# Joined q/k/v/dO loads, two PSUM copies moved from ACT to DVE, a delayed tail, and stores issued two jobs behind their transposes

## The chip, the cores and the metric

The kernel runs on one core of a Trainium2 chip. The metric is the device time of one execution in microseconds; the table below gives the median of several runs and the time of the one execution that the profiler recorded. The engines are PE (matmul), DVE (vector), ACT (scalar), POOL and SP. SP computes nothing here: it issues DMAs, in order. POOL and, at the start and the end, ACT issue DMAs as well. Work moves between engines by semaphores, and every engine runs its own list in order.

## The reference

The reference computes the sum of a residual, a self-attention block and a SwiGLU block, all on the same layer-normalised input, and then the gradients of everything for a given output gradient. With S = 2048 rows, D = 448 columns, H = 16 heads of 28 and F = 1792:

```python
xn = layernorm(x)                                   # (2048, 448)
q, k, v = split(xn @ wqkv)                          # 16 heads of 28
p = softmax(q @ k.T * 28 ** -0.5)                   # per head 2048 x 2048
A = merge(p @ v) @ wo
B = (silu(xn @ w_gate) * (xn @ w_up)) @ w_down
y = x + A + B
# outputs: y and, for grad_out, the gradients of x, wqkv, wo, w_gate, w_up, w_down
```

## The kernel before

The program has three stages, each with an order of work that is written out by hand.

**Forward stage.** Heads are padded from 28 to 32 rows, so that four heads make a group of 128 partitions and there are G = 4 groups. The loop runs over 256 steps (group, 512 query columns, 128 key rows). In each step PE makes the scores of four heads (L599), ACT takes the exponential (L604), and PE multiplies the one of the step before with v (L581). What time PE has left is filled by `fill(pace)`, which takes small pieces of work from a queue of jobs (`queue`, `cur`): the SwiGLU block and its backward (`ffn_items`), the weight gradients (`dW_items`), the projections of the next group (`proj_items`), and what follows a finished block of outputs (`o_items`). Each piece has a cost, and the pace is the cost that is left divided by the steps that are left. `push(..., front=True, behind=n)` puts jobs into the queue behind its first n jobs.

Many results are needed in a second layout. It is made by a transposing DMA, which SP issues (`sp.dma_start_transpose`), mostly followed by a store to a DRAM buffer. The store waits for the transpose to land. In `o_items` the store of oT is issued by SP right behind its transpose (L493), and the stores of dOT (L524) and of the weight gradients dw_o (L370, L371) are issued by POOL right behind theirs. While an engine's queue waits for a landing, all that is behind it in that queue waits too: on SP the next transposes, on POOL the stores of the SwiGLU rows (L421) and the weight loads of the next block (L161). `proj_done` stores q, k and v transposed into `qT_d`, `kT_d` and `vT_d`, one store of 128 rows each.

**Backward stage.** Heads are taken in NPR = 8 pairs. There are N = 512 units (pair, 512 keys, 128 queries). A window is eight units that share keys, called by W; the place in the window is `pos`, 0 to 7, and the place of a unit is `qi`. In the step of unit k, PE makes the scores of unit k (L851, tile sd), then the products of dO and v of unit k-1 (L862, also sd). ACT makes E of unit k (L869), DVE makes ds of unit k-1 out of sd and E (L880). There are three sd buffers, so the scores of unit k wait for ds of unit k-3, and L862 of unit k waits for E of unit k. Three units late, `acc_mm` (L748) adds up the gradients of k and v. They are taken out by ACT at the end of every second window (dkv_o, L754).

The gradient of q needs ds with queries in the columns (dsT). Of the eight units of a window six are transposed by DMA (L882), and the two in `TQ = (1, 4)` by PE (`pe_transpose`, L775) into the PSUM bank aux: the first at pos 6, copied out by DVE (`tr_out(dve)`, L782), the second at pos 0 of the next window, copied out by ACT (`tr_out(act)`). A ds tile has eight buffers, so the product of unit k may not be written before the readers of unit k-8 are done, its transposing DMA among them.

The aux bank exists once and is passed round. In each window it also takes one *job*: a row block of the output ("y", 19 matmuls), of the gradient of the normalised input ("dx", 14 matmuls), or a part of a weight gradient ("dwq"). The job's matmuls (the `fillers`) are spread over pos 1 to 4, and ACT takes the result out (L727, L691). At pos 5 `dq_mm` (L795) uses the bank for the gradient of q of two windows ago, and DVE takes this out at pos 6 (`dq_out`, L807, L810, L813).

SP's queue in this stage holds the six transposes of a window, two row loads (ck and, for y, x_c) at pos 0, the transposes of dkv_o and dq_o, and the loads of the next pair, the next group and the next weights at pos 4: up to two of the lists `pload` and `wload` and one of `gload` per window. `load_pair` fills the tiles of a pair in half-height pieces: q (rows 0 to 63 of a tile) from `qT_d`, dO (rows 64 to 127 of the same tile) from `dOT_d`, and in the same way k and v. In the loop each piece is half a row long as well, so a pair takes eight loads.

**Tail.** For each of 16 row blocks PE adds up the gradient of the normalised input (14 matmuls, L956 and L958), ACT and DVE make the two sums of the layer norm's backward (L962, L965), and then t1 (ACT, L974), t2 (DVE, L976) and the sum with the residual gradient (POOL, L979), which SP stores (L980).

Of the kernel before, what the change touches and what calls it, by code (L numbers as in the profile page):

```python
# [37 lines left out]
def kernel(  # L38
# [27 lines left out]
    qT_d = dram.tile([G, P, S], BF16, name="qT_d")  # L66
    kT_d = dram.tile([G, P, S], BF16, name="kT_d")
    vT_d = dram.tile([G, P, S], BF16, name="vT_d")
    dOT_d = dram.tile([G, P, S], BF16, name="dOT_d")
# [128 lines left out]
    def proj_done(g):  # L198
# [5 lines left out]
        pool.dma_start(out=vT_d[g], in_=vT[:])  # L204
        pool.dma_start(out=qT_d[g], in_=qT[:])
        pool.dma_start(out=kT_d[g], in_=kT[:])
# [120 lines left out]

    def proj_items(g):
# [15 lines left out]
    def dW_items(fc):  # L344

        out = []
        for wi in range(3):
            box = {}

            def go(t, wi=wi, box=box):  # L350
# [13 lines left out]
                else:  # L364
# [5 lines left out]
                    pool.dma_start(out=dst[0:384].rearrange("(c p) f -> p c f", p=P), in_=o[:, 0:3, :])  # L370
                    pool.dma_start(out=dst[384:448], in_=o[:64, 3, :])  # L371
# [94 lines left out]
    def o_items(g, qc, o_ps):  # L466
# [8 lines left out]
        def tr(i):  # L475
# [3 lines left out]
            if i < 3:  # L479
# [13 lines left out]
            sp.dma_start(out=hd_d[tsl, :, g, :].rearrange("k p s -> p k s"),  # L493
                         in_=oT[:].rearrange("p (k s) -> p k s", k=4))

        def do(i):
# [27 lines left out]
            pool.dma_start(out=dOT_d[g, :, qc * 512:(qc + 1) * 512], in_=dT[:])  # L524
# [20 lines left out]
    def load_pair(pr, parts):  # L545

        g, r = pr // 2, 64 * (pr % 2)
        q = qkp.tile([P, S], BF16, name="qT")
        k = qkp.tile([P, S], BF16, name="kT")
        qd[pr] = (q, k)  # L550
        n = S // parts
        return [lambda i=i, dst=dst, r0=r0, src=src: sp.dma_start(
                    out=dst[r0:r0 + 64, i:i + n], in_=src[g, r:r + 64, i:i + n])
                for r0, srcs in ((0, (qT_d, kT_d)), (64, (dOT_d, vT_d)))
                for dst, src in zip((q, k), srcs) for i in range(0, S, n)]
# [212 lines left out]
    TQ = (1, 4)  # L768
# [9 lines left out]
    def tr_out(eng):  # L778

        ps, dst = st["tr"]  # L780
        out, in_ = dst.rearrange("p j c q -> p (j c) q"), ps[:]
        act.copy(out=out, in_=in_) if eng is act else dve.tensor_copy(out=out, in_=in_)  # L782
# [47 lines left out]
    for k in range(N + 2 * UW):  # L830
        W, pos = k // UW, k % UW
        if k < N:
# [7 lines left out]
            if pos == 4:  # L840
                if W == len(jobs) - 1:
                    wload.extend(load_w("wq", 2))
                for lst, n in ((pload, 2), (gload, 1), (wload, 2)):
# [10 lines left out]
        late_tr = pos == 0 and 1 <= W <= NW  # L854
# [15 lines left out]
        if late_tr:  # L870
            tr_out(act)
# [15 lines left out]
        if pos == 1:  # L887
            if 3 <= k < N + 3:
                acc_mm(k - 3)
            if job:  # L890
                st["aux"] = ps_x.tile([P, 512], FP32, name="aux")
# [120 lines left out]
```

## Time and profile before

| | |
|---|---|
| median of 3 runs | 1534.82 us (1529.53 to 1534.94) |
| the profiled execution | 1534.68 us |
| its span, first to last instruction | 1532.9 us |
| mean granted PE clock over the span | 0.979 |
| PE busy | 1414.2 us (92%) |
| ACT busy | 1187.9 us (77%) |
| DVE busy | 1100.7 us (72%) |
| POOL busy | 395.0 us (26%) |
| first and last product ds | 644.8 and 1455.4 us |

Three kinds of lines are used below. A group line has the source line, the engine, the operation, `out<-in` by the program's names, the count, and busy times; what stands in brackets or at the end is the idle time ahead of it and what ended that. A line of the order of time has start and length in us first. A line of a window view has the window, its length, the busy time and count of each engine, the granted share of PE's clock, the mean busy share of the 16 DMA engines and the GB/s that they moved. Rows with SPq are times in which SP issued a DMA.

### The profile page before, as it was taken

What the parts mean: (1) busy time and instruction counts of PE and PEld (TensorE: products, weight loads), DVE (VectorE), ACT (ScalarE), POOL (GpSimd) and SP (SyncE); (2) the same over time, 40 slices, a digit from 0 to 9 for tenths busy, and PEclk for the clock granted to TensorE, in tenths of its full rate; (3) what the DMA queues carried; (4) which work ended last, traced back from release to release, by engine and by line L of the source; (5) the groups of instructions that cost most, each with busy time, mean ns of one, the idle gap of its engine ahead of it and who ended that gap; (6) DMA issues with size and microseconds to landing.
All of it is one profiled execution on the core that took longest, in us unless ns stands there. A gap on an engine that the chain in (4) does not pass through costs nothing.

```text
span 1532.9 us, 32019 instructions
## 1 busy us (share of the span) xinstructions
PE 1414.2 (92%) x12176; PEld 600.1 (39%) x12176; DVE 1100.7 (72%) x1421; ACT 1187.9 (77%) x1333; POOL 395.0 (26%) x664
## 2 busy tenths in 40 slices
PE   6899999999999999798989988989899899999987
PEld 3233333333333333333334344334345343544353
DVE  7664555656666667377878878888788788888925
ACT  6898998889888888576767777778778778788823
POOL 4332443344435444400111121101112101111033
PEclk9999999999999999889999999999999999999999
DMA  9976767878877799799999999999999999999984
GB/s 216 190 157 144 156 122 157 171 136 169 173 166 144 159 190 214 178 197 208 218 206 207 185 194 209 197 204 206 208 195 197 198 205 183 180 190 211 186 272 140
DMA packets 682106, 285.12 MB, mean 186 GB/s; under 512 B 637136, under 2 KB 650464, under 8 KB 681952
## 3 DMA queue, kind: packets, MB, share of 16 engines
q1 hardware_dynamic: 652016, 210.03, 75.5%
q0 software_dynamic: 25968, 64.53, 17.2%
q10 hardware_dynamic: 3968, 8.52, 1.7%
q8 instruction: 95, 1.56, 0.4%
q14 instruction: 59, 0.48, 0.1%
HBM read 67.34 MB, written 63.44 MB: 85 GB/s over the span
## 4 chain that ended last, share of the span: by engine, by line
PE 59%; ACT 13%; DMA 12%; DVE 8%; issue 6%; POOL 1%; SPq 0%; DVEq 0%; ACTq 0%; POOLq 0%
DMA dsT<-ds 9%; PE f_ps L356 8%; PE s_ps L599 7%; PE f_ps L382 7%; PE sd L851 6%; ACT E L869 5%; PE aux L718 5%; PE acc L748 4%; PE o_ps L581 4%; ACT eT L604 4%; PE aux L775 4%; DVE ds L880 4%; PE aux L795 3%; ACT dsT L782 3%; PE f_ps L180 3%
## 5 line engine op out<-in xcount | busy, mean ns | idle before, releaser
L880 DVE TENSOR_TENSOR ds<-sd,E 128x1024 bf16<-128x1024 f32 x512 | 611.5, 1219 | 134.0 <-PE sd L862 49.8
L869 ACT ACTIVATE E<-sd 128x1024 bf16<-128x1024 f32 x512 | 516.7, 1023 | 175.6 <-PE sd L862 136.5
L604 ACT ACTIVATE eT<-s_ps 128x1024 bf16<-128x1024 f32 x512 | 497.2, 1025 | 79.5 <-PE s_ps L599 76.1
L862 PE MATMUL sd<-kT,qT 32*128 32x512 bf16 x1024 | 203.4, 390 | 22.2 <-ACT E L869 21.3
L851 PE MATMUL sd<-kT,qT 32*128 32x512 bf16 x1024 | 202.7, 392 | 20.6 <-DVE ds L880 18.0
L748 PE MATMUL acc<-ds,v_sp 128*32 128x512 bf16 x1024 | 205.3, 396 | 0.7 <-DVE ds L880 0.7
L748 PE MATMUL acc<-E,O_sp 128*32 128x512 bf16 x1024 | 205.1, 396 | 0.2 <-ACT dkv_o L754 0.2
L599 PE MATMUL s_ps<-qT,kT 32*128 32x512 bf16 x1024 | 152.8, 383 | 10.1 <-ACT eT L604 7.9
L421 POOL DMA_DIRECT2D hd_d<-fT x168 | 126.9, 773 | 18.5 <-DVE fT L416 5.3
L382 PE MATMUL f_ps<-xnT,wgu 128*128 128x512 bf16 x448 | 117.6, 381 | 1.7 <-DVE w_sb L408 1.5
L763 POOL DMA_DIRECT2D dqkv_d<-dkv_o x64 | 39.2, 616 | 293.3 <-ACT dkv_o L754 291.4
L718 PE MATMUL aux<-W,ck 128*128 128x448 bf16 x448 | 107.5, 357 | 3.3
L851 PEld LDWEIGHTS <-qT 32*128 32x128 bf16 x1024 | 51.2, 91 | 150.0 <-issue 141.2
L581 PE MATMUL o_ps<-eT,v_sp 128*32 128x512 bf16 x1024 | 102.8, 391 | 0.0
L356 PE MATMUL f_ps<-xn_sp,f_sp 128*128 128x448 bf16 x448 | 99.7, 356 | 0.0
L599 PEld LDWEIGHTS <-kT 32*128 32x128 bf16 x1024 | 42.4, 90 | 143.5 <-issue 136.8
L748 PEld LDWEIGHTS <-O_sp 128*32 128x32 bf16 x1024 | 50.3, 93 | 113.5 <-issue 104.0
L775 PE MATMUL aux<-ident_bf,ds 128*128 128x128 bf16 x1024 | 81.3, 224 | 13.5 <-DVE dq_acc L807 6.5
L356 PEld LDWEIGHTS <-f_sp 128*128 128x128 bf16 x672 | 58.3, 98 | 78.6 <-issue 23.5
L862 PEld LDWEIGHTS <-qT 32*128 32x128 bf16 x1024 | 65.2, 91 | 60.5 <-issue 56.5
L775 PEld LDWEIGHTS <-ds 128*128 128x128 bf16 x1024 | 63.5, 99 | 42.4 <-issue 41.7
L394 DVE SCALAR_TENSOR_TENSOR g<-t_sb,f_ps 128x512 f32<-128x512 f32 x56 | 38.4, 686 | 54.0 <-ACT t_sb L392 53.9
(133 smaller groups left out, 1763.1 us busy)
## 6 DMA issues: line engine op xcount, KB each, us to landing
hd_d<-fT POOLq DMA_DIRECT2D x168, 128.0 KB, 4.6
ck<-hd_d SPq DMA_DIRECT2D x32, 448.0 KB, 4.3
ck<-hd_d SPq DMA_DIRECT2D x16, 576.0 KB, 4.9
dsT<-ds SPq DMA_TRANSPOSE x384, 4.2
dqkv_d<-dkv_o POOLq DMA_DIRECT2D x64, 64.0 KB, 3.8
dq_c<-dqkv_d ACTq DMA_DIRECT2D x5, 768.0 KB, 6.1
W<-wT_d SPq DMA_DIRECT2D x14, 224.0 KB, 3.6
out_dram<-dw_o POOLq DMA_DIRECT2D x28, 96.0 KB, 3.7
```

The costliest lines, as they stand in the source:

```text
L356: pe.matmul(acc[:, :D], lhsT=src[:, 12 * (t // 4) + 4 * wi + t % 4, :], rhs=rhs[:, t, :D], start=(t == 0), stop=(t == NT - 1))
L382: pe.matmul(st[name][:], lhsT=w(c), rhs=src[:, tsl, c, :], start=(c == 0), stop=(c == 3))
L581: pe.matmul(o_ps[HP * hh:HP * (hh + 1), :], lhsT=v[:, kt, HP * hh:HP * (hh + 1)], rhs=e[hh // 2][:, hh % 2, :], start=(kt == 0), stop=(kt ...
L599: pe.matmul(s_ps[:, j, :], lhsT=kT[r:r + HP, kt * P:(kt + 1) * P], rhs=qT[r:r + HP, qc * 512:(qc + 1) * 512], start=True, stop=True, tile_ ...
L604: act.activation(out=e[:], in_=s_ps[:], func=ACT.Exp, scale=SCALE)
L718: return [lambda n=n: pe.matmul(ps[:, :D], lhsT=t[:, n, :], rhs=w[:, n, :], start=(n == 0), stop=(n == NFC - 1)) for n in range(NFC)]
L748: pe.matmul(acc[r:r + HP, :], lhsT=src[:, qt, 64 * hp + HP * j:64 * hp + HP * j + HP], rhs=m[:, j, :], start=(qt == 0), stop=(qt == NT - 1 ...
L775: pe.transpose(ps[:, i, :], ds[:, i // 4, (i % 4) * P:(i % 4 + 1) * P], ident_bf[:])
L851: pe.matmul(s_ps[:, j, :], lhsT=q[HP * j:HP * j + HP, qt * P:(qt + 1) * P], rhs=kv[HP * j:HP * j + HP, kc * 512:(kc + 1) * 512], start=Tru ...
L862: pe.matmul(d_ps[:, j, :], lhsT=q[r:r + HP, qt * P:(qt + 1) * P], rhs=kv[r:r + HP, kc * 512:(kc + 1) * 512], start=True, stop=True, tile_p ...
L869: act.activation(out=E[k][:], in_=s_ps[:], func=ACT.Exp, scale=SCALE)
L880: dve.tensor_tensor(out=DS[k - 1][:], in0=d_ps[:], in1=E[k - 1][:], op=ALU.mult)
```

## The change

The change has four parts.

1. *Loads.* The buffers `qT_d` and `dOT_d` become one, `qdo_d`, with a tile of 128 rows for each pair (64 of q, 64 of dO); `kT_d` and `vT_d` become `kv_d`. A pair is then loaded by four full-height loads instead of eight. The stores that fill the buffers are split by pairs: `proj_done` issues six instead of three, and dOT takes two instead of one. In the loop, a window of even number issues one load of a pair, one of odd number one load of a group.
2. *Copies.* The units that PE transposes are 2 and 6. Both results are copied out by DVE: the first at pos 7 behind that step's product, the second at pos 1 ahead of that step's product. The job starts at pos 2 instead of 1, so its matmuls are spread over three positions; at pos 2 they stand behind `acc_mm`, and at pos 5 `acc_mm` stands ahead of `dq_mm`.
3. *Forward stores.* The stores of oT, dOT and dw_o become jobs of cost 0 that are pushed behind the first two jobs of the queue.
4. *Tail.* t2, the addition and the store of row block t-1 are issued behind the sums of row block t, and the last three additions are made by DVE.

```diff
-        pool.dma_start(out=vT_d[g], in_=vT[:])
-        pool.dma_start(out=qT_d[g], in_=qT[:])
-        pool.dma_start(out=kT_d[g], in_=kT[:])
+        for hp in range(2):
+            rows = slice(64 * hp, 64 * hp + 64)
+            for dst, src in ((kv_d[2 * g + hp, 64:], vT), (qdo_d[2 * g + hp, :64], qT), (kv_d[2 * g + hp, :64], kT)):
+                pool.dma_start(out=dst, in_=src[rows, :])
...
+    def store_later(f):
+        push([[(0.0, f)]], front=True, behind=2)
...
-                    pool.dma_start(out=dst[0:384].rearrange("(c p) f -> p c f", p=P), in_=o[:, 0:3, :])
-                    pool.dma_start(out=dst[384:448], in_=o[:64, 3, :])
+                    def store():
+                        pool.dma_start(out=dst[0:384].rearrange("(c p) f -> p c f", p=P), in_=o[:, 0:3, :])
+                        pool.dma_start(out=dst[384:448], in_=o[:64, 3, :])
+                    store_later(store)
...
-            sp.dma_start(out=hd_d[tsl, :, g, :].rearrange("k p s -> p k s"),
-                         in_=oT[:].rearrange("p (k s) -> p k s", k=4))
+            store_later(lambda: sp.dma_start(out=hd_d[tsl, :, g, :].rearrange("k p s -> p k s"),
+                                             in_=oT[:].rearrange("p (k s) -> p k s", k=4)))
...
-            pool.dma_start(out=dOT_d[g, :, qc * 512:(qc + 1) * 512], in_=dT[:])
+            def store():
+                for hp in range(2):
+                    pool.dma_start(out=qdo_d[2 * g + hp, 64:, qc * 512:(qc + 1) * 512],
+                                   in_=dT[64 * hp:64 * hp + 64, :])
+            store_later(store)
...
-        return [lambda i=i, dst=dst, r0=r0, src=src: sp.dma_start(
-                    out=dst[r0:r0 + 64, i:i + n], in_=src[g, r:r + 64, i:i + n])
-                for r0, srcs in ((0, (qT_d, kT_d)), (64, (dOT_d, vT_d)))
-                for dst, src in zip((q, k), srcs) for i in range(0, S, n)]
+        return [lambda i=i, dst=dst, src=src: sp.dma_start(out=dst[:, i:i + n], in_=src[pr, :, i:i + n])
+                for i in range(0, S, n) for dst, src in ((q, qdo_d), (k, kv_d))]
...
-    TQ = (1, 4)
+    TQ = (2, 6)
...
-                for lst, n in ((pload, 2), (gload, 1), (wload, 2)):
+                for lst, n in ((pload, 1 - W % 2), (gload, W % 2), (wload, 2)):
...
-        late_tr = pos == 0 and 1 <= W <= NW
+        late_tr = pos == 1 and 1 <= W <= NW
...
         if late_tr:
-            tr_out(act)
+            tr_out()
...
-        if pos == 1:
-            if 3 <= k < N + 3:
-                acc_mm(k - 3)
-            if job:
-                st["aux"] = ps_x.tile([P, 512], FP32, name="aux")
-                fillers = job_mms(W, st["aux"])
-        if 1 <= pos < 5 and job:
+        if pos == 7 and W < NW:
+            tr_out()
+        acc = 3 <= k < N + 3
+        if pos == 2 and job:
+            st["aux"] = ps_x.tile([P, 512], FP32, name="aux")
+            fillers = job_mms(W, st["aux"])
+        lump = []
+        if 2 <= pos < 5 and job:
             n = -(-len(fillers) // (5 - pos))
-            for f in fillers[:n]:
-                f()
-            fillers = fillers[n:]
+            lump, fillers = fillers[:n], fillers[n:]
+        if acc and pos == 2:
+            acc_mm(k - 3)
+        for f in lump:
+            f()
+        if acc and pos != 2:
+            acc_mm(k - 3)
...
-        if pos != 1 and 3 <= k < N + 3:
-            acc_mm(k - 3)
...
             pe_transpose(W, TQ[0])
-            tr_out(dve)
...
+        def finish(t, t1, cc):
+            t2 = wk.tile([P, D], FP32, name="t2")
+            dve.scalar_tensor_tensor(out=t2[:], in0=xn_sp[:, t, :D], scalar=cc[:, 0:1], in1=t1[:],
+                                     op0=ALU.mult, op1=ALU.add)
+            dx = wk.tile([P, D], BF16, name="dx")
+            add = pool if t < NT - 3 else dve
+            add.tensor_tensor(out=dx[:], in0=t2[:], in1=dy_t[:, t, :], op=ALU.add)
+            sp.dma_start(out=out1_d[:, t, :], in_=dx[:])
...
-            t2 = wk.tile([P, D], FP32, name="t2")
-            dve.scalar_tensor_tensor(out=t2[:], in0=xn_sp[:, t, :D], scalar=cc[:, 0:1], in1=t1[:],
-                                     op0=ALU.mult, op1=ALU.add)
-            dx = wk.tile([P, D], BF16, name="dx")
-            pool.tensor_tensor(out=dx[:], in0=t2[:], in1=dy_t[:, t, :], op=ALU.add)
-            sp.dma_start(out=out1_d[:, t, :], in_=dx[:])
+            if t > 0:
+                finish(t - 1, *held)
+            held = (t1, cc)
+        finish(NT - 1, *held)
```

More of the change, by code (lines that the diff above doesn't have):

```diff
@@ L65 @@
     dram = ctx.enter_context(tc.tile_pool(name="dram", bufs=1, space=DRAM))
[L66 to L69, printed above, removed]
+    qdo_d = dram.tile([2 * G, P, S], BF16, name="qdo_d")
+    kv_d = dram.tile([2 * G, P, S], BF16, name="kv_d")
     spq_d = dram.tile([G, P, NT * P], BF16, name="spq_d")
@@ L545, in load_pair @@
     def load_pair(pr, parts):
-        g, r = pr // 2, 64 * (pr % 2)
         q = qkp.tile([P, S], BF16, name="qT")
@@ L776, in pe_transpose, with tr_out @@
         st["tr"] = (ps, dsT[:, :, :, qi * P:(qi + 1) * P])
-    def tr_out(eng):
+    def tr_out():
         ps, dst = st["tr"]
-        out, in_ = dst.rearrange("p j c q -> p (j c) q"), ps[:]
-        act.copy(out=out, in_=in_) if eng is act else dve.tensor_copy(out=out, in_=in_)
+        dve.tensor_copy(out=dst.rearrange("p j c q -> p (j c) q"), in_=ps[:])
     def dq_mm(W, half):
```

## The prediction

> **What bounds the kernel now.** I read the page first (busy shares, the chain that ended last), then windows by stage, then the waits of the stage with most to lose, and there the order of time of SP, DVE, PE and ACT.
>
> ```profile
> PE 1414.2 (92%) x12176; PEld 600.1 (39%) x12176; DVE 1100.7 (72%) x1421; ACT 1187.9 (77%) x1333; POOL 395.0 (26%) x664
> PE 59%; ACT 13%; DMA 12%; DVE 8%; issue 6%; POOL 1%; SPq 0%; DVEq 0%; ACTq 0%; POOLq 0%
> ```
> ```profile
> 100.00:600.00 500.00, 489.62 (x3284) 186.18 (x3283) 310.35 (x536) 442.38 (x491) 207.16 (x302) 1.00 0.80 162
> ```
> The forward stage has PE busy 489.6 of 500 us: little can be won there. The backward stage (643 to 1455 us) is different. The next windows count the DVE product of L880, eight of which make one window of the loop (columns: length, DVE busy and count, granted clock, DMA share, GB/s).
>
> ```profile
> 643.00:869.00 226.00, 160.49 (x135) 0.95 1.07 205
> 831.30:868.80 37.50, 28.69 (x25) 1.00 1.10 196
> 869.00:1241.00 372.00, 277.04 (x233) 0.98 1.08 201
> 1241.00:1444.00 203.00, 162.84 (x137) 0.99 1.10 190
> ```
> The last row is a quiet stretch: 17 windows in 203 us, 11.94 us each. The 29 windows of 869 to 1241 took 372 us; at the quiet rate 346, so 26 us are lost. The 17 windows up to 869 carry the longer output rows ("y"); three undisturbed ones took 37.5 us, 12.5 each, and at that rate 226 would be 212.5: 13.5 lost. Together 39 us. The clock column shows part of what a stall costs: 0.95 and 0.98 where there are stalls, 0.99 to 1.00 where there are none. What the stalls are, the waits tell; the first row is of 643 to 869, the second of 869 to 1241, the third of 1241 to 1444:
>
> ```profile
> DVE ds L880 <- DMA dsT<-ds: 24.5, 16, 2.9
> ...
> DVE ds L880 <- DMA dsT<-ds: 21.6, 16, 3.6
> ...
> DVE ds L880 <- DMA dsT<-ds: 0.5, 1, 0.5
> ```
> DVE may not write a new ds tile before the transposing DMA that reads the tile's buffer of eight units ago has landed. The transposes are late because SP, which issues them, is never free. The worst place, SP and then DVE:
>
> ```profile
> 1099.89 1.23 SPq L761 DMA_TRANSPOSE dkv_sp<-dkv_o  x1
> 1101.17 1.22 SPq L552 DMA_DIRECT2D qT<-dOT_d  x2
> 1102.44 0.58 SPq L563 DMA_DIRECT2D vT<-spk_d  x1
> 1103.12 4.62 SPq L882 DMA_TRANSPOSE dsT<-ds  x3
> 1107.84 0.94 SPq L666 DMA_DIRECT2D ck<-hd_d  x1
> ```
> ```profile
> 1107.99 2.35 DVE L880 TENSOR_TENSOR ds<-sd,E 128x1024 bf16<-128x1024 f32 x2 [3.65 <-DMA dsT<-ds]
> ```
> Every SP row begins where the one before ends. So SP's issue time, beside PE, DVE and ACT, limits the disturbed windows, and in the quiet ones it just keeps up.
>
> **The change, part by part.** The profiled execution took 1534.68 us, of which 1532.9 are span; the median of the runs is 1534.82, so the sum below serves for both.
>
> *Joined loads.* A pair's q and k tiles came by eight half-height loads in the loop and come by four full-height ones; bytes and row lengths stay. Price of one issue:
>
> ```profile
> L552 SPq DMA_DIRECT2D qT<-qT_d x15: 470/587/1521, 558.4 to 1275.5; - x15
> L552 SPq DMA_DIRECT2D kT<-vT_d x15: 581/588/1977, 576.9 to 1311.0; - x15
> ```
> ```profile
> L882 SPq DMA_TRANSPOSE dsT<-ds x384: 1231/1292/5342, 653.0 to 1458.9; - x192
> ```
> Seven pairs times four is 28 issues fewer, at 0.59 us 16.5 us of SP. They also come thinner: at most one load of pair or group a window, where up to three stood in a row (1101.17 to 1103.02 above, 1.8 us ahead of the transposes that DVE then waited for). A full-height load may take longer to issue; no row shows one from these tensors, but the 128-row group load of the same width at 1102.44 took 0.58, so I take 0.59. The transposes by DMA stay 384, and their 1.29 us each, six a window, 7.75 us, stay the bulk of SP's work; unit 2 and 6 go by PE where it was 1 and 4, so SP meets runs of three (7, 0, 1 and 3, 4, 5) instead of four and two, which lowers the backlog at no cost. Of the 39 us lost I take half, 19.5: the 16.5 us of issues and a little for the spreading. Bounds: 0, if the transposes alone keep SP late, and 39. Weight loads (two a window, as before) can still collide near 881 to 930 and 1139 to 1190 us, which is why I don't take all.
>
> A rule of the Trainium skill bears on this (DMA: Bandwidth & Descriptors, Rules for kernel authors): transfers to two partition halves run on the same 16 engines anyway, so one should use one 128-partition transfer, and issuing from several queues saves sequencer time only. By the rule alone a kernel held up by the DMA engines would gain nothing from the joining, and that term would be 0. The trace speaks for the sequencer: the DMA share is highest, 1.10, just where no transpose is waited for.
>
> *The window's order of work.* Rows of a quiet window, PE, then DVE, then ACT:
>
> ```profile
> 1380.13 1.15 PE L795 MATMUL aux<-dsT,vT 128*32 128x512 bf16 x16
> 1382.12 0.61 PE L775 MATMUL aux<-ident_bf,ds 128*128 128x128 bf16 x8
> 1384.16 0.39 PE L862 MATMUL sd<-kT,qT 32*128 32x512 bf16 x2 [0.19 <-ACT E L869]
> 1386.20 0.92 PE L718 MATMUL aux<-W,ck 128*128 128x448 bf16 x4
> 1388.31 0.39 PE L748 MATMUL acc<-E,O_sp 128*32 128x512 bf16 x2
> 1388.65 0.39 PE L851 MATMUL sd<-kT,qT 32*128 32x512 bf16 x2
> 1392.10 1.15 PE L795 MATMUL aux<-dsT,vT 128*32 128x512 bf16 x16
> ```
> ```profile
> 1381.38 0.68 DVE L813 SCALAR_TENSOR_TENSOR dq_o<-aux,dq_acc 128x512 bf16<-128x512 f32 x1
> 1381.98 1.21 DVE L880 TENSOR_TENSOR ds<-sd,E 128x1024 bf16<-128x1024 f32 x1
> 1383.11 0.68 DVE L782 COPY dsT<-aux 128x1024 bf16<-128x1024 bf16 x1
> 1383.71 3.47 DVE L880 TENSOR_TENSOR ds<-sd,E 128x1024 bf16<-128x1024 f32 x3
> ```
> ```profile
> 1385.14 1.01 ACT L782 COPY dsT<-aux 128x1024 bf16<-128x1024 bf16 x1
> 1388.77 0.69 ACT L754 ACTIVATE dkv_o<-acc,sc_col 128x512 bf16<-128x512 f32 x1 [0.26 <-PE acc L748]
> ```
> One PSUM bank, aux, is passed round the window: dq, first transposes, second transposes, job, dq. In these rows dq starts 1380.13, dq_o 1.25 later, the job's matmuls 4.82 after that (held by ACT's copy, which ends at 1386.15), and the next dq 5.90 after them: 11.97 us.
>
> After: from dq_o DVE does dq_o (0.60 to the next start), two products (1.13 apart, from three in 3.47), the first copy (0.60), a product, the second copy. PE's second transposes wait for the first copy and for the score matmuls behind an E, as at 1384.16; I place the second copy's end at 5.3 and the job's start at 5.5, 0.7 later than before. The job's 14 matmuls (0.19 apart: four in 0.92 less the last one's 0.35) then need 2.65 and 0.3 of changeovers, with three score and three acc groups (0.33 each, 1388.31 to 1388.65), 4.9 instead of 5.9, since one step fewer lies between and ACT's 0.69 for dkv_o, now behind an acc that goes ahead of the job, falls into a gap. With 1.25 for dq that is 11.65: 0.3 us less than 11.97. "y" windows push 19 matmuls into three steps instead of four; the same working gives 12.6 against 12.5. DVE takes 0.60 more (the copy), ACT 1.01 less. DVE's own work becomes 8 x 1.13 + 3 x 0.60 = 10.85 of that: no slack to speak of beyond 0.8. And SP has no room for windows much shorter than 11.94. So I take 0.08 a window, 5 us over 64; bounds are -19 (0.3 in all) and +38 (the copy's 0.60 in full, 64 times).
>
> VectorE: DVE Perf Modes of the Trainium skill (Specifications) says that ScalarE sits closer to PSUM, which speaks against giving DVE the copies. Here the same copy took 0.68 us on DVE and 1.01 on ACT; by the rule's direction one would keep it on ACT, and the sum would lose this term's gain.
>
> *Forward stores.* The store of oT is no longer ahead of the transpose of dOT on SP, the stores of dw_o and dOT are issued later on POOL.
>
> ```profile
> 602.36 3.65 SPq L491 DMA_TRANSPOSE oT<-O_sp  x1
> 611.40 0.37 SPq L493 DMA_DIRECT2D hd_d<-oT  x1
> 611.88 1.19 SPq L522 DMA_TRANSPOSE dOT<-dOl  x1
> ```
> ```profile
> 624.84 1.30 PE L356 MATMUL f_ps<-dy_sp,f_sp 128*128 128x448 bf16 x3 [5.00 <-DMA f_sp<-fT]
> ```
> Between 606.01 and 611.40 SP sat behind that store. Now dOT goes in this gap and what follows comes 1.3 us earlier, among it the transpose that PE awaited for 5.00 us. In the other 15 places PE is covered by its own backlog (489.6 of 500). Gain 1.5 us; bounds 0 and 5. Added on POOL: per group six stores instead of three, and two of dOT for one: 12 + 16 = 28 issues.
>
> ```profile
> 31.79 0.58 POOL L204 DMA_DIRECT2D vT_d<-vT  x1 [18.49 <-DVE vT L193]
> ```
> 28 x 0.58 = 16 us on an engine that is busy 207 of 500 us. Behind them queue the stores that free fT and the next block's weight loads, hidden under PE; without that cover they would cost the 16.
>
> *Tail.* DVE's t2 of one row follows the next row's sums, and the last three additions go to DVE.
>
> ```profile
> 1528.48 0.69 DVE L976 SCALAR_TENSOR_TENSOR t<-xn_sp,cc,t 128x448 f32<-128x448 bf16 x1 [0.85 <-ACT t L974]
> 1529.24 1.03 POOL L979 TENSOR_TENSOR dx<-t,dy_t 128x448 bf16<-128x448 f32 x1 [1.70 <-DVE t L976]
> ```
> ```profile
> 1522.00:1533.00 11.00, 1.05 (x6) 0.34 (x4) 4.62 (x13) 3.22 (x7) 3.18 (x4) 0.71 0.13 42
> ```
> PE is done with its last row about 1.1 us after 1522; the remaining 10 us are one row's ACT and DVE steps, queued behind the row before, POOL's 1.03 and the store. Taking t2 off the way to the next sums (0.69, two rows deep) and a DVE addition of about 0.6 for 1.03 with its hand-over gives 2 to 5 us; I take 4. Were the addition slower on DVE, 1 would be left.
>
> Sum: 1534.7 - 19.5 - 5 - 1.5 - 4 = 1504.7, so **1505 us**.
>
> **Rivals.** (a) *SP stays late.* The 384 transposes, not the loads, keep SP full (7.75 us a window at the median, with dkv, dq and row loads over 10), so the stalls come at other places and the shorter order finds no room: only forward and tail remain, 1534.7 - 5.5 = 1529. For it: SP's rows without gaps. Against: the quiet stretch with the same transposes has 0.5 us of such waits.
>
> (b) *DVE becomes the bound* (slower). In the four steps from dq_o on DVE has four products and three evacuations, 6.3 us, while PE has little; if PE can't run ahead, the 0.60 of the second copy is paid in every window: +38, against 25 saved in the rest: 1534.7 + 38 - 25 = 1548. It decides from 25 / 64 = 0.39 us a window on. For it: DVE gets the copy exactly between products that run back to back (1383.71, three in 3.47). Against: DVE waited for PE in the job's steps, where the lag is made up.
>
> (c) *Both terms in full*: 1534.7 - 39 - 12 - 1.5 - 4 = 1478; the 12 is 0.25 in the 46 windows after 869. For it: most stalls also cost clock. Against: SP's floor.
>
> **Chances.** Forecast (1488 to 1523) 0.55, (a) 0.15, (b) 0.18, (c) 0.12. A measurement of this kernel can tell about 0.5% from no change, 7.7 us. Faster: forecast, (c) and a little of (a), 0.69; same: the rest of (a) with small forms of (b), 0.14; slower 0.17. The range leaves out the far half of (b) and most of (c): 1484 to 1540.
>
> **What would show it.** Right: the wait of ds for dsT falls from some 46 us to under 25, and 869 to 1241's counterpart has windows near 12.2; quiet windows of 11.6 to 11.9 with no copy on ACT; last addition on DVE and the span ending under 9 us after PE's last row. Wrong: DVE busy above 95% with PE waiting for ds or for the copies (b), or unchanged waits for dsT (a). The working fails most easily at the place where I let the second copy end 5.3 us after dq_o.

## The result and the profile after

The changed kernel took 1516.38 us (median of four runs, 1510.25 to 1521.93); the kernel before, on the same chip, 1533.2. The ratio is 0.9892, with a 95% interval of 0.9847 to 0.9938: 16.8 us were won, where the sum had 30. The profiled execution took 1518.61 us, of which 1516.5 are span. Of two kernels below (whole stores, the jobs' loads on POOL) some executions, one of ten and three of twelve, fell in a slower state; their medians are of all executions, their ratios of the others.

I read the two traces by three stages, cut at the first and the last exponential E on ACT (us, the profiled executions):

| stage | before | after | difference | forecast |
|---|---|---|---|---|
| start to first E (forward) | 643.7 | 650.6 | +6.9 | -1.5 |
| first E to last E (backward) | 809.9 | 791.5 | -18.4 | -24.5 |
| last E to the end (tail) | 79.2 | 74.4 | -4.8 | -4 |

The forward stage is longer in two places. These are PE's waits of over 2 us for a DMA in the order of time, from 34 us to the first E. The first row is of the kernel before:

```profile
69.65 0.93 PE L356 MATMUL f_ps<-dy_sp,f_sp 128*128 128x448 bf16 x2 [3.65 <-DMA f_sp<-fT]
```
and these are of the changed kernel:

```profile
56.94 0.61 PE L388 MATMUL f_ps<-dyT,wdT 128*128 128x512 bf16 x1 [5.54 <-DMA dyT<-dy_sp]
...
632.27 1.30 PE L359 MATMUL f_ps<-dy_sp,f_sp 128*128 128x448 bf16 x3 [8.96 <-DMA f_sp<-fT]
```
Before, the second place is the wait of 5.00 us that the prediction shows; it was to shrink by 1.3 and grew by 4. The first place was in no part of the sum.

In the backward stage, the waits by releaser of DVE after (total, times, longest):

```profile
DVE ds L886 <- DMA dsT<-ds: 34.9, 34, 2.7
DVE ds L886 <- PE sd L868: 32.9, 63, 3.2
```
The wait for dsT was 46.6 us before and is 34.9 after, not under 25. The 29 windows that correspond to 869 to 1241 took 361.2 us, 12.5 each, where 12.2 was named. The quiet windows became as short as worked out. The first row shows two of them, from the windows of all engines (length, PE, PEld, DVE, ACT, POOL busy, granted clock, DMA share, GB/s), the others show the two copies on DVE between products in one of them:

```profile
1384.00:1407.00 23.00, 21.91 (x222) 8.91 (x220) 22.16 (x23) 17.49 (x20) 2.37 (x4) 1.00 1.11 205
```
```profile
1384.81 0.68 DVE L788 COPY dsT<-aux 128x1024 bf16<-128x1024 bf16 x1
1385.40 1.22 DVE L886 TENSOR_TENSOR ds<-sd,E 128x1024 bf16<-128x1024 f32 x1
1386.53 0.68 DVE L788 COPY dsT<-aux 128x1024 bf16<-128x1024 bf16 x1
```
That is 11.5 us a window, with DVE busy 22.16 of 23.00. The second copy ended 5.4 us after the start of the row that takes dq out (1381.81), where the prediction placed it at 5.3 and thought itself weakest. But in this pair of profiles the stretch in which these windows stand hardly gained: from window 47 on the stage lasted 200.9 us before and 200.3 after, since two windows of it (47 and 50, 11.8 and 12.0 us before) now took 12.8 and 13.2, and the last one 11.5 instead of 9.9. The joined loads, from the list of one tile's operations (min/median/max ns):

```profile
L562 SPq DMA_DIRECT2D qT<-qdo_d x15: 529/570/769, 567.6 to 1311.6; - x15
...
L562 SPq DMA_DIRECT2D kT<-kv_d x15: 551/571/577, 575.2 to 1336.2; - x15
```
A full-height load takes SP no longer to issue (0.57 us at the median) than a half-height one (0.587).

### The profile page after: what moved, and what is told of

It reads as the page before. It is cut to its first block, busy times and chain, and to the rows that moved or that the text cites. A ratio compares the mean times of both kernels' runs of the same rounds, so it can differ in the third digit from the quotient of the medians.

```text
span 1516.5 us, 31830 instructions
## 1 busy us (share of the span) xinstructions
PE 1393.2 (92%) x12176; PEld 580.0 (38%) x12176; DVE 1129.2 (74%) x1488; ACT 1129.3 (74%) x1269; POOL 407.5 (27%) x689
## 4 chain that ended last, share of the span: by engine, by line
PE 66%; DVE 11%; DMA 10%; ACT 9%; issue 4%; SPq 0%; DVEq 0%; ACTq 0%
PE f_ps L359 8%; PE sd L857 7%; PE s_ps L607 7%; PE f_ps L388 7%; DMA dsT<-ds 6%; PE acc L756 6%; DVE ds L886 5%; PE aux L726 5%; ACT E L875 4%; PE o_ps L589 4%; ACT eT L612 4%; PE aux L783 4%; PE aux L720 4%; PE sd L868 3%; PE f_ps L178 3%
## 5 line engine op out<-in xcount | busy, mean ns | idle before, releaser
L886 DVE TENSOR_TENSOR ds<-sd,E 128x1024 bf16<-128x1024 f32 x512 | 612.0, 1219 | 80.5 <-DMA dsT<-ds 34.9
L607 PE MATMUL s_ps<-qT,kT 32*128 32x512 bf16 x1024 | 152.4, 384 | 10.2 <-ACT eT L612 8.1
L726 PE MATMUL aux<-W,ck 128*128 128x448 bf16 x448 | 101.4, 355 | 0.0
L788 DVE COPY dsT<-aux 128x1024 bf16<-128x1024 bf16 x128 | 87.2, 681 | 0.7 <-PE aux L783 0.7
```

The costliest lines, as they stand in the source:

```text
L607: pe.matmul(s_ps[:, j, :], lhsT=kT[r:r + HP, kt * P:(kt + 1) * P], rhs=qT[r:r + HP, qc * 512:(qc + 1) * 512], start=True, stop=True, tile_ ...
L726: return [lambda n=n: pe.matmul(ps[:, :D], lhsT=t[:, n, :], rhs=w[:, n, :], start=(n == 0), stop=(n == NFC - 1)) for n in range(NFC)]
L886: dve.tensor_tensor(out=DS[k - 1][:], in0=d_ps[:], in1=E[k - 1][:], op=ALU.mult)
```

## The experiments

My theory after the result: the loads' issue time on SP carries the backward gain, the order of the window a little; the forward loss comes from the six half stores at 32 to 36 us and from the deferred stores at the stage's end. Rivals: the order is all of the gain; the forward loss is a difference between runs.

**The loads alone.** The kernel before with the joined tensors, their stores and the new counts per window:

```diff
-                for lst, n in ((pload, 2), (gload, 1), (wload, 2)):
+                for lst, n in ((pload, 1 - W % 2), (gload, W % 2), (wload, 2)):
```


> The kernel before with the joined and thinner loads alone (full-height tensors q/dO and k/v, six half stores per group and two per dOT piece, at most one pair or group load a window). Three stages are read: from the start to the first E, from the first E to the last E, and from the last E to the end; before they took 643.7, 810 and 79 us, after 650.6, 791.5 and 74. Theory: SP's issue time is what the loads cost, so the backward stage loses 8 to 15 us (to 795-802) by 16 us less of loads on SP, and the wait of ds for dsT falls from 46.6 to about 30 us; the six half stores on POOL make the forward stage about 3 us longer, near 50 us. Rival (SP stays late): the transposes alone keep SP full, the backward stage stays within 4 us of 810 and the wait of ds for dsT above 42 us. Rival (the forward loss is only a difference between runs): the forward stage stays within 1 us of 643.7.

Measured: 1517.45 us, ratio 0.9898 (0.9865 to 0.9932), that is 15.6 us less than before. The forward stage took 645.3 us, the backward stage 799.3. So the joined loads alone win nearly as much as the whole change does. Of the rival that SP stays late regardless, one sign failed (a backward stage within 4 us of 810) and one came (a wait for dsT above 42 us), for the wait of DVE for dsT did not fall:

```profile
DVE ds L878 <- DMA dsT<-ds: 57.1, 49, 3.0
DVE ds L878 <- PE sd L860: 45.0, 102, 1.6
```
It is 57.1 us where it was 46.6, in a stage 10.6 us shorter. In the kernel with the forward stores alone (below), whose backward stage is that of before to the letter, the same wait is

```profile
DVE ds L887 <- DMA dsT<-ds: 61.5, 46, 3.4
```
So this total differs by 15 us between two executions of the same code (46.6 and 61.5), and neither its rise nor its fall by that much tells anything. What went in this pair of profiles were waits behind other names (for E 12.6 to 5.2 us, for sd 49.8 to 45.0, copies and rows) and some of PE's busy time (746 to 740 us, at a granted clock of 0.97 before and 0.98 here). By what path the joined loads shorten the stage is not shown.

**The order of the window alone.** The kernel before with part 2 of the change:

```diff
-    TQ = (1, 4)
+    TQ = (2, 6)
...
-        late_tr = pos == 0 and 1 <= W <= NW
+        late_tr = pos == 1 and 1 <= W <= NW
...
-            tr_out(act)
+            tr_out()
```


> The kernel before with the new order of the window alone (transposes by PE of units 2 and 6, both copies on DVE, the job in three steps, acc ahead of it). Theory: the quiet windows after 1240 us go from 11.95 to about 11.5 us, the backward stage shortens by 5 to 10 us, and the loads, which still come three in a row, keep the wait of ds for dsT above 35 us. Rival (the order is all of it): the backward stage falls to 793 or less, as in the changed kernel. Rival (DVE becomes the bound): windows of 12.5 us and a backward stage over 815 us. Forward stage and tail within 1 us of before.

Measured: 1533.18 us, ratio 0.9989 (0.9959 to 1.0018): no change that can be told, between 6 us less and 3 more. The quiet windows are 11.5 us, as in the changed kernel, and the stage of the profiled execution is 802.8 us, but that execution (1527.98) was 5 us under the median. The 5 us that the prediction gave this part lie inside the interval. The rival that the order is all of it falls, and so does the one that DVE becomes the bound.

**The forward stores alone.** The stores of oT and dw_o are put off in the same way:

```diff
+    def store_later(f):
+        push([[(0.0, f)]], front=True, behind=2)
...
-            pool.dma_start(out=dOT_d[g, :, qc * 512:(qc + 1) * 512], in_=dT[:])
+            store_later(lambda: pool.dma_start(out=dOT_d[g, :, qc * 512:(qc + 1) * 512], in_=dT[:]))
```


> The kernel before with the forward stores two jobs behind alone (oT, dOT, dw_o). Theory: the loss at the end of the forward stage (PE's wait for f_sp 8.96 us in the changed kernel, 5.00 before) comes from these, so the first E is at 646 to 648 us, all of it lost after 610 us; the step near 50 us is as before. Rival (the gain that was forecast): first E at 641 to 643 us. Rival (half stores do it all): first E within 1 us of 643.7. Backward stage and tail as before.

Measured: 1552.62 us, ratio 1.0118 (1.0079 to 1.0158), 18 us more than before, far more than any theory had. The place is the one expected; SP, POOL and PE in the order of time, and the DMA issues from 614 to 620 us (count, KB, median us from issue to landing):

```profile
614.87 4.82 SPq L425 DMA_TRANSPOSE f_sp<-fT  x1
```
```profile
616.61 1.10 POOL L546 DMA_DIRECT2D W<-in_B_w_down_dram  x1
```
```profile
638.82 1.30 PE L360 MATMUL f_ps<-dy_sp,f_sp 128*128 128x448 bf16 x3 [17.71 <-DMA f_sp<-fT]
```
```profile
W<-in_B_w_down_dram POOLq DMA_DIRECT2D x1, 1568.0 KB, 21.8
f_sp<-fT SPq DMA_TRANSPOSE x1, 23.9
```
POOL, SP and the landing in the same place of the kernel before:

```profile
614.80 0.56 POOL L524 DMA_DIRECT2D dOT_d<-dOT  x1 [9.74 <-DMA dOT<-dOl]
...
619.53 0.74 POOL L370 DMA_DIRECT2D out_dram<-dw_o  x1 [1.41 <-DMA dw_o<-dwT]
...
623.05 1.10 POOL L539 DMA_DIRECT2D W<-in_B_w_down_dram  x1
```
```profile
616.36 3.89 SPq L418 DMA_TRANSPOSE f_sp<-fT  x1
```
```profile
f_sp<-fT SPq DMA_TRANSPOSE x1, 8.4
```
There the stores of dOT and dw_o held POOL, 9.74 and 1.41 us, and it reached the load of W, 1568 KB, 6.7 us after SP began to issue the last f_sp transpose (616.36). With the stores put off, POOL is there 1.7 us after, the load and the transpose are under way together, and the transpose lands 23.9 us after its issue instead of 8.4. The transpose itself was issued 1.5 us earlier than before (614.87 against 616.36), as the prediction had said. POOL's waits had been a brake that something else needed. This is read from the order of time: no run moves the load of W alone in this kernel, which lost the 18 us.

**Whole stores.** The six half stores of a group are issued as three, each over both halves' rows of the joined tensor, and the two of a dOT piece as one:

```diff
-            for dst, src in ((kv_d[2 * g + hp, 64:], vT), (qdo_d[2 * g + hp, :64], qT), (kv_d[2 * g + hp, :64], kT)):
-                pool.dma_start(out=dst, in_=src[rows, :])
+        for dst, src in ((kv_d[2 * g:2 * g + 2, 64:], vT), (qdo_d[2 * g:2 * g + 2, :64], qT), (kv_d[2 * g:2 * g + 2, :64], kT)):
+            pool.dma_start(out=dst, in_=src[:])
```


> The changed kernel with the stores for the joined tensors issued whole again (three per group and one per dOT piece, each writing both halves' rows of the joined tensor); the loads stay joined. Theory: the 5.54 us of PE waiting for dyT near 51 us go, the lag there falls from 4.2 to 1 us or less, the first E comes 3 to 4 us earlier (646.5 to 647.5), backward stage and tail stay, 1513 us in all. Rival (the wait for dyT comes from the run, not from the number of stores): first E within 1 us of 650.6.

Measured: 1546.16 us, ratio 1.0081 (1.0048 to 1.0113), 30 us more than the changed kernel. Both theories missed: the edit has a cost of its own. DMA issues from 30 to 40 us, first of this kernel, then of the changed one:

```profile
kv_d<-vT POOLq DMA_DIRECT2D x1, 512.0 KB, 21.5
qdo_d<-qT POOLq DMA_DIRECT2D x1, 512.0 KB, 23.8
```
```profile
kv_d<-vT POOLq DMA_DIRECT2D x2, 256.0 KB, 7.4
qdo_d<-qT POOLq DMA_DIRECT2D x2, 256.0 KB, 8.2
```
A store to a destination of the form 2 x 64 x 2048 lands in 21 to 24 us, where two of 64 x 2048 land in 7 to 8. DMA: Bandwidth & Descriptors of the Trainium skill (Rules for kernel authors) gives a reason: the slowest dimension larger than one sets how many DMA engines serve a transfer, so one of size 2 confines it to at most two. The trace agrees in the direction, threefold the time; no view here shows the engines of one transfer. The packets differ as well: from 30 to 40 us POOL's queue moved 0.29 MB in 2343 packets, in the changed kernel 0.76 MB in 220, so the cause of the slow stores stays open. PE waited 10.77 us for dyT here. So the number of stores was not tested by this run, only that dyT is late when these stores are slow.

**Three edits of the forward stage.** First the stores undone in the changed kernel:

```diff
     def store_later(f):
-        push([[(0.0, f)]], front=True, behind=2)
+        f()
```


> The changed kernel with the forward stores issued at once again (store_later calls its argument); everything else as changed. In the run with the forward stores alone PE waited 17.7 us for f_sp at the end of the forward stage against 5.0 before, and the load of W (1568 KB) was issued 1.7 us after that f_sp transpose against 6.7 before. Theory: the stores of dw_o, which wait for the landing of their transposes, used to hold POOL's queue and with it that load back; here the load is issued 6 us or more behind the f_sp transpose again, the wait is 5 to 6 us, the first E comes 3 to 5 us earlier (645.5 to 647.5; lag at step 248 still 3 to 4 us), and the time is 1511 to 1513 us. Rival (the two waits differ by the run, not by the order of stores): first E within 1 us of 650.6.

then its load of W put later:

```diff
-        if fc == 13:
-            ffn_list.append([(0.0, lambda: load_w("wd", 1)[0]())])
...
-    ffn_list += last + pend
+    ffn_list += last + pend[:1] + [[(0.0, lambda: load_w("wd", 1)[0]())]] + pend[1:]
```


> The changed kernel with its late stores, but with the load of W (the forward-to-backward weight, 1568 KB) put behind the first of the last three dW jobs, so that POOL issues it once that job is done, when f_sp has landed. Theory (the load's bytes delay the f_sp transpose): the last f_sp transpose lands within 9 us of its issue (13.7 in the changed kernel, 23.9 with the forward stores alone), PE's wait for it is under 5.5 us, the first E comes 4 to 6 us earlier (644.5 to 646.5), and the backward stage stays within 5 us of 791.5 since the first use of W is some 30 us later. Rival (the stores themselves, not the load, delay it): the wait stays at 8 us or more.

then the first group's stores put later:

```diff
+        if g > 0:
+            proj_store(g)
...
+    push([[(0.0, lambda: proj_store(0))]], front=True, behind=30)
```


> The changed kernel with the six half stores of the first group (kv_d, qdo_d) issued 30 jobs into the forward stage instead of at its start, ahead of nothing that is waited for. Theory: these stores (32.8 to 36 us) delay the last dyT transpose through the DMA engines; without them PE's wait for dyT (5.54 us) is under 1 us, the lag at step 16 against before falls from 4.3 to between -3 and 0 us, the first E comes 4 to 7 us earlier. Rival (dyT is late for the transposes ahead of it on SP): wait within 1.5 us of 5.54.

and both of the last two together:

> The changed kernel with both edits, the load of W behind the first of the last dW jobs and the first group's stores 30 jobs later. Theory: the two add, first E at 638 to 643 us, the backward stage as in the changed kernel, 1504 to 1509 us, 0.5 to 0.8% below the changed kernel. Rival (time won in the forward stage is given back in the backward stage, since its first loads wait for the load of W): 1514 us or more.

| kernel | W issued after f_sp | f_sp lands after | PE's wait for it | first E | time, ratio |
|---|---|---|---|---|---|
| before | 6.7 | 8.4 | 5.00 | 643.7 | 1533.2 |
| forward stores alone | 1.7 | 23.9 | 17.71 | 657.8 | 1552.62, 1.0118 |
| changed | 3.1 | 13.7 | 8.96 | 650.6 | 1516.38, 0.9892 |
| stores undone | 6.5 | 8.4 | 4.72 | 647.2 | 1515.02, 0.9876 (0.9849 to 0.9903) |
| W later | 16.3 | 10.2 | 5.61 | 648.8 | 1513.94, 0.9877 (0.9850 to 0.9904) |
| group 0 late | 3.8 | 10.2 | 6.42 | 642.1 | 1502.67, 0.9797 (0.9773 to 0.9821) |
| both later | 14.0 | 7.3 | 1.12 | 634.4 | 1502.09, 0.9781 (0.9763 to 0.9800) |

(us; the first two columns are from the issue of the last f_sp transpose.) At the ends of the column the load of W goes with the landing: 1.7 us behind, 23.9; over 6 us behind, 7.3 to 10.2. With the load put late and the stores kept late the wait is 5.61 instead of 8.96. In between the run decides: three more kernels below have the changed kernel's forward stage to the letter, their loads of W come 2.9 to 3.3 us behind, as its own does, and their waits were 2.31, 6.88 and 5.34 us. So the 8.96 was partly a matter of the run, and in the time of the whole kernel neither of the first two edits can be told from the changed kernel. The run with W later also missed its own marks (a landing within 9 us, a wait under 5.5, the first E by 646.5), so how much the load costs at 3 us behind stays open; for its cost at 1.7 us one kernel stands. The kernel with whole stores (5.2 us behind, landing after 14.3) is not in the table, since its slow stores lie on POOL's queue too.

The stores of group 0 are another matter. With them put off there is no wait for dyT, nor the wait for f_sp near 70 us that the kernel before had; the first E comes 8.5 us earlier than in the changed kernel, where 4 to 7 were expected, and the time falls by 13.7 us (1502.67). In the seven kernels whose stores of group 0 go out at once as six halves, the waits for dyT are 5.54, 4.61, 7.08, 5.64, 5.01, 2.96 and 0.87 us; with three stores, as before, there is no wait for dyT but one of 2 to 4 us for f_sp. Read at the first exponential of step 16 of the forward loop (67.7 us with the stores late, 71.2 on the mean of three kernels with three stores, 73.6 on the mean of the seven), three stores at the start cost 3.5 us and six halves 6. Both edits together give 1502.09 us, 2.2% under the kernel before and more than was expected: a version that beats both the kernel before and the changed one. Against group 0 alone it gained nothing that can be told: the forward stage is 7.7 us shorter, the backward stage was 5.3 longer, in two executions.

**The spreading undone** (joined loads, but again up to two pair loads and one group load a window):

```diff
-                for lst, n in ((pload, 1 - W % 2), (gload, W % 2), (wload, 2)):
+                for lst, n in ((pload, 2), (gload, 1), (wload, 2)):
```


> The changed kernel with up to two pair loads and one group load in each window again, as before; the loads stay joined. Theory (fewer issues carry the gain, the spreading a little): the backward stage grows by 0 to 5 us (791.5 to 797) and the time is 1516 to 1521 us. Rival (the spreading carries it): 800 us or more in the backward stage and 1525 us or more.

Measured: 1517.7 us, ratio 0.9899 (0.9869 to 0.9928), backward stage 793.2. The spreading is worth nothing that can be told; the joining carries it.

**The order undone** in the changed kernel, the second experiment backwards:

```diff
-    TQ = (2, 6)
+    TQ = (1, 4)
...
-        late_tr = pos == 1 and 1 <= W <= NW
+        late_tr = pos == 0 and 1 <= W <= NW
```

> The changed kernel with the old order of the window (transposes by PE of units 1 and 4, second copy on ACT, job in four steps). Theory: the order was worth about 5 us of the time: quiet windows of 11.9 to 12.0 us, 1519 to 1524 us. Rival (the order is worth nothing in the whole, as in the run with the order alone, whose median was 0.1% under before): 1514 to 1518 us. Rival (the order pays only once the loads are thin): 1526 us or more.

Measured: 1515.32 us, ratio 0.9883 (0.9857 to 0.9908). The quiet windows are back at 11.8 to 12.0 us, and the median is no longer. With the run of the order alone this says twice that 0.45 us less in a quiet window, 29 us by 64, is not found again in the whole. Whether a part of it is, such as the 5 us of the prediction, the two runs can't tell: 5 us lie within the noise of both. The profiles speak for some gain. The backward stage is 800.4 us here and 791.5 in the changed kernel, and it was 809.9 before and 802.8 with the order alone; but the execution profiled here was 6.6 us over its median and the one with the order alone 5.2 under. From window 47 on the stage took 200.8 to 203.3 us in the four kernels with the old order, 201.9 on the mean, and 196.9 to 201.9 in the eight with the new one, both copies on DVE and the jobs' loads on SP, 199.2 on the mean.

**The second copy on ACT.**

```diff
         if late_tr:
-            tr_out()
+            tr_out(act)
```


> The changed kernel with the second copy of the window on ACT instead of DVE, at the same place in the order. Theory (the copy's length on the way to the job counts, 1.01 us on ACT against 0.68): quiet windows go from 11.5 to 11.7-11.9 us, 1520 to 1530 us. Rival (DVE is the bound in these windows, so 0.60 us less of it is won): quiet windows of 11.0 to 11.3 us, 1505 to 1512 us. Rival (neither): 11.5 and within 3 us of 1516.

Measured: 1511.94 us, ratio 0.9887 (0.9842 to 0.9932). Quiet windows took 11.8 and 12.0 us, about as my theory had them, and again there is no loss of time. The median lies 4.4 us under that of the changed kernel, so none of the three forecasts came whole: the first had the windows, the second the time, the third missed both. The intervals of the two kernels overlap; which engine takes the copy makes no difference that can be told here.

**The jobs' loads on POOL**, in the best kernel, to relieve SP further:

```diff
-    def job_load(i):
+    def job_load(i, q=sp):
...
-                job_load(W + 2)
+                job_load(W + 2, pool)
```


> The kernel with both forward edits (1502 us) and the loads of the jobs' chunks (ck, x_c; 64 issues that took 38 us of SP in the backward stage) issued by POOL instead of SP. Theory (SP's issue time still costs the disturbed windows): the wait of ds for dsT falls from 48.8 us to under 38, the backward stage from 795 to 783-790, the time is 1490 to 1497 us. Rival (SP's freed time is taken by longer issues of the transposes, since the DMA engines behind them are the limit): backward stage within 4 us of 795 and 1499 to 1505 us. Rival (POOL issues the loads too late for the jobs): over 1507 us, with PE waiting for ck.

Measured: 1544.11 us, ratio 1.0058 (1.0034 to 1.0082), 42 us more than the same kernel with these loads on SP. It is over 1507, but not by PE's waiting for ck, which comes to 0.9 us. The wait of ds for dsT rose from 48.8 to 77.7 us. POOL, SP and DVE around the worst place:

```profile
773.92 0.56 POOL L672 DMA_DIRECT2D ck<-hd_d  x1
774.47 0.56 POOL L674 DMA_DIRECT2D x_c<-in_A_x_dram  x1
```
```profile
774.99 0.95 SPq L575 DMA_DIRECT2D O_sp<-spo_d  x1
776.03 12.08 SPq L892 DMA_TRANSPOSE dsT<-ds  x3
788.16 1.26 SPq L827 DMA_TRANSPOSE dq_sp<-dq_o  x1
```
```profile
786.31 1.22 DVE L890 TENSOR_TENSOR ds<-sd,E 128x1024 bf16<-128x1024 f32 x1 [7.29 <-DMA dsT<-ds]
```
Three transposes take SP 12.08 us, four each, right behind loads of 576 and 112 KB on POOL's queue and one of 256 KB (O_sp) on SP's own. In the kernel with the loads on SP three transposes behind such a pair of loads take 7.18, 2.4 each:

```profile
773.17 0.53 SPq L672 DMA_DIRECT2D ck<-hd_d  x1
773.79 0.38 SPq L674 DMA_DIRECT2D x_c<-in_A_x_dram  x1
774.27 7.18 SPq L892 DMA_TRANSPOSE dsT<-ds  x3
```
Over the stage SP issued 38 us less of loads, but the transposes' rows grew from 597 to 670 us and the stage from 795 to 836. So a row of SP is not a fixed price: a transpose took it 1.3 us at the median, and four here. That the row lasts until the DMA engines take the work is how I read this; no view shows it.

## Why the prediction was right, and where not

The kernel became faster, inside the range and on the side that had 0.69. Of the 30 us of the sum 16.8 came, near the slow end of the range: in the pair of profiles the forward stage lost 6.9 us, where 1.5 were to be won, and the backward stage won 18.4, where 24.5 were. By terms:

*Joined loads, -19.5.* Measured alone -15.6 (-20.7 to -10.4). SP's rows for the pair loads went from 38.8 us to 18.0 with the loads alone and 15.9 in the changed kernel; the 16.5 of the working was 20.8 and 22.9. The transposes' rows grew from 581.6 us to 597.0 and 594.5, so part of the relief was taken back. So the cause, the joining, is shown and its size was near, but the path was argued: less issue time was to mean less waiting for dsT, and with the loads alone that wait was no shorter (57.1 us, against 46.6 and 61.5 with the old loads). That the size came near is partly luck. That the term is SP's issue time alone isn't shown either: the joined load of 256 KB also lands as soon as the half one of 128 KB did (3.2 to 3.5 us against 3.1 to 3.8), so fewer issues and fewer transfers under way came together. The bytes did not change: 162.0 MB in 450 thousand packets in the backward stage, before and with the loads alone. The "little for the spreading" was nothing that can be told. The rule of the Trainium skill that I set against the term (DMA: Bandwidth & Descriptors, Rules for kernel authors) was right in its first half, one transfer of full height instead of two, though not for a gain of 0; its second half, that several queues save the sequencer's time only, is too mild here: another queue lost 42 us.

*Window order, -5.* Measured alone -1.7 (-6.3 to +2.8), and nothing that can be told when it was undone; 5 is neither shown nor excluded. The working of the single window held: 11.5 us in quiet windows, where 11.65 was worked out, 12.5 in "y" windows, where 12.6 was. The 0.45 us did not carry over to 64 windows, and the prediction, which wrote "SP has no room", was right to take only a small part. A reason that fits, not shown: SP's issues fill 91 to 93% of the backward stage in all the kernels run, 730 of 792 us after, 11.4 for each window, about as long as a quiet window of 11.5, so windows that run ahead of SP may give it back in a later one. As a row of SP stretches, that 11.4 is no firm floor. Rival (b), DVE as the bound, didn't come: DVE's busy time grew by 33 us in the stage, but its waits for sd fell from 49.8 to 32.9. Of (b)'s sign, DVE busy above 95%, the quiet windows have the number (22.16 of 23.00, 96%), but they became shorter.

*Rival (a)* was right that SP stays as full as it was (92% of the stage before and after) and wrong in its conclusion: the joined loads pay all the same.

*Forward stores, -1.5.* This step was wrong. Alone they cost 18 us; in the changed kernel undoing them moved nothing that can be told. Two steps failed. The transpose did come earlier alone (by 1.5 us, where 1.3 was said), but the load of W came 6.4 us earlier too, and the transpose then landed after 23.9 us instead of 8.4. And of the 28 issues on POOL "hidden under PE" the first six stand at a place at which PE is not covered, and dyT came late; with them put off the time fell by 13.7 us. The cover was read from 100 to 600 us and used for 32 and 620.

*Tail, -4.* The tail is 4.8 us shorter in the pair of profiles. Over all of them it is 77.9 us on the mean of the four with the old tail and 74.9 of the ten with the new, 3.0 less. It was not run alone, but its end is the same in every profile: from PE's last matmul to the end of the span 9.8 to 10.1 us in the four, 7.0 to 7.1 in the ten. The additions moved to DVE took 0.63 us, where 0.6 was assumed, and the last steps stand close together:

```profile
1511.63 0.63 DVE L964 TENSOR_TENSOR dx<-t,dy_t 128x448 bf16<-128x448 f32 x1
1512.17 0.68 DVE L960 SCALAR_TENSOR_TENSOR t<-xn_sp,cc,t 128x448 f32<-128x448 bf16 x1
1512.89 0.63 DVE L964 TENSOR_TENSOR dx<-t,dy_t 128x448 bf16<-128x448 f32 x1
```

The terms don't add: -15.6, -1.7, +18 and -3 make -2, the changed kernel has -16.8. The loss by the stores seems to depend on where the load of W falls against one transpose, and the other parts moved that from 1.7 to 3.1 us. Of the signs that I named, the quiet windows and the tail came as said, and the windows of 869 to 1241 half (12.5, for 12.8 before and 12.2 said); the wait for dsT under 25 us didn't, and was the wrong sign to name.

What stays open: by what path the joined loads shorten the backward stage, how much of their gain is SP's time and how much the DMA engines', and whether the window's order is worth some 5 us or nothing. Of the 13.7 us of group 0's stores the profiles show 8.5 in the forward stage and 1.7 in the backward one; the two profiled executions differ by 10.7 us, and the rest lies between executions.

## What to carry to other kernels

Before a store or a load is moved, list what its queue's next large transfer is: a wait that looks idle may be what keeps that transfer off a transpose on which an engine depends. In this kernel a queue full of DMA transposes gained from fewer and taller loads in the same queue (15.6 us) and lost when other loads were moved to a queue beside it (42 us); try both before believing either. A shorter quiet window need not shorten the stage by its difference times the count; look for an engine or a queue whose mean time per window is as long. And read a cover such as PE's backlog at the place where it is used, not in the middle of the stage.

## What the hardware showed that I had not expected

Transposes on SP's queue were slow where large transfers ran on POOL's: one f_sp transpose landed after 8.4 us with a load of 1568 KB started 6.7 us behind it and after 23.9 with it started 1.7 us behind, where that load took 21.8 us to land. Transposes of ds took 4 us of SP each beside a 576 KB load on POOL's queue and 2.4 behind such a load on SP's own, against 1.3 at the median. DMA: Bandwidth & Descriptors of the Trainium skill (Queues, rings and completion order) says that each DMA engine goes round the queues packet by packet. The packets here differ in size: the queues of the changed kernel, with packets, MB and the share of 16 engines' span:

```profile
q1 hardware_dynamic: 651536, 210.03, 77.0%
q0 software_dynamic: 26416, 64.53, 18.2%
```
SP's have 322 bytes on the mean and POOL's 2443. If what the profile counts as packets are the page's, which nothing here shows, a turn each would give POOL's queue the larger part of the bytes. That fits the slowing; no run here varied the packet size.
